# Raw w1 blocks of the first pair loaded into free x buffers, two units ahead and in program order

## The chip, the cores and the metric

The kernel runs on one core of a Trainium2 chip. A core has four engines that compute, each with a queue of its own that it works through in order: TensorE (PE, the matrix products; PEld is its weight load), VectorE (DVE), ScalarE (ACT) and GpSimd (POOL). A fifth, SyncE (SP), issues the transfers between HBM and the on-chip memory here. An engine waits at an instruction until what it reads is there and what it writes to is free, and everything behind that instruction waits with it. The metric is the device time of one execution in microseconds.

## The reference

Attention over 4 batches, 8 heads, 768 positions of 64: each query sees keys within 16 positions and 24 block summaries. Its output is laid out as 3072 tokens of 512, and goes through a mixture of four experts:

```python
p = domain_probs / (domain_probs.sum(-1, keepdims=True) + 1e-09)
for e in range(E):
    h = np.maximum(x @ w1[e], 0.0)
    out += p[:, e:e + 1] * (h @ w2[e])
```

w1 is 4 x 512 x 1024, w2 is 4 x 1024 x 512, all float32. The change concerns the loading of w1 alone.

## The kernel before

Tokens are worked in eight blocks of 384. Attention for a later block is interleaved with the experts of an earlier one. Blocks 0 and 1 go through the experts in plain products; blocks 2 to 7 go in three pairs (`PAIRS`, L926), each through all four experts, the first pair in the order 3, 2, 1, 0. In a pair the first layer of an expert (`first`, L1177) runs in four units i = 0 to 3, each with two raw blocks of w1 of 128 x 512 float32. A unit is a scheme of seven groups of six products (`SEVEN`, L1037) that write four banks of PSUM: a, d, b, a, b, c, b. Between the groups ACT copies bank a into bank b (`phb<-pha`, L1215), ACT copies d to a helper p5 (L1218), and DVE makes c (`phc`, L1220) and adds p5 to d. The second layer (`po`) of the expert ahead is interleaved with the first layer of the next; the first expert of the pair has none behind it, only attention.

The weights of a unit are made ready by `w1_operands` (L817). In the first pair it loads the two raw blocks (`wr1<e>_<block>`, by `load_weights`, L740), scales both on ACT (the page shows `one`), makes seven operands from them, each with a high part (a cast to half precision on ACT) and a low part (a subtraction on POOL or DVE), with sums between them on POOL, into two groups w1g0 and w1g1, and puts stores of both groups to HBM on a list that is issued eight units later. In the second and third pair these stored operands are loaded instead, and no raw block is touched. `fetch` (L941) walks a list of all units of all pairs and calls `w1_operands`; `first` calls it for its own unit and for the one after. `w2_scaled` (L777) does the like for w2, also with two raw blocks at a time (`wr2<e>_<block>`).

The raw blocks of w1 and of w2 share four buffers (tag `wr`). The tag `x` has 14 buffers (`NX`) of the same size. While blocks 0 and 1 run, they hold the inputs of the plain products and pieces of attention; a pair's seven operands of x take seven of them.

A scheduler sets the order of the instructions on each engine from a simulated timeline; PSUM evictions in `first` have a raised priority (`RUSH`). Loads on SP float in this order too, but for those of attention's summaries, which are pinned to the order of the program (`load_chunk`, L201, with `tc.keep_in_program_order`). In names of the profile numbers are left out: `wr` is a raw block of either layer, and its DMA names its source, `in_w1L` or `in_w2L`.

Of the kernel before, what the change touches and what calls it, by code (L numbers as in the profile page):

```python
# [8 lines left out]
F32 = mybir.dt.float32  # L9
# [7 lines left out]
P = 128  # L17
# [26 lines left out]
NX = 14  # L44
# [18 lines left out]
def attn_moe(ctx: ExitStack, tc: tile.TileContext, qvL, qv0, v0L, kD, kT, vT, w1L, w2L, dpL, cst, out):  # L63
    nc = tc.nc
# [20 lines left out]
    def pool(name, bufs=1, **kw):  # L85
        return ctx.enter_context(tc.tile_pool(name=name, bufs=bufs, **kw))
# [7 lines left out]
    sb = pool("sb")  # L94
# [645 lines left out]
    def load_weights(src, e, fc, which):  # L740
        raw = sb.tile([P, 512], F32, name=f"wr{which}{e}_{fc}", tag="wr", bufs=4)
        SP.dma_start(raw, src[e, fc])
        return raw

    def w1_parts(name, n, dtype=F32R):
        return sb.tile([P, n, 512], dtype, name=name, tag="w1", bufs=NW1)
# [5 lines left out]
    stored = {}  # L752
# [4 lines left out]
    def later(units, issue, *a):  # L757
        deferred.append([units, issue, a])
# [54 lines left out]


    WS = ("11", "s1", "s2", "12"), ("s3", "s4", "22")

    def w1_operands(e, pr):  # L817
        groups = [w1_parts(f"w1g{j}{e}_{pr}", len(names), F16) for j, names in enumerate(WS)]
        ws = {w: groups[j][:, n, :] for j, names in enumerate(WS) for n, w in enumerate(names)}
        if (e, pr, "1") in stored:  # L820
            for to, kept_in in zip(groups, stored[e, pr, "1"]):
                SP.dma_start(to, kept_in)
            return ws
        r1, r2 = (load_weights(w1L, e, 2 * pr + j, "1") for j in range(2))
        for raw in (r1, r2):
            A.mul(raw, raw, scale_w[e][0])
        a11, a12 = r1[:, 0:256], r1[:, 256:512]
        a21, a22 = r2[:, 0:256], r2[:, 256:512]
        def parts(w, raw, lo):
            hi, low = ws[w][:, 0:256], ws[w][:, 256:512]  # L830
            A.copy(hi, raw)
            lo.tensor_tensor(low, raw, hi, op=ALU.subtract)

        parts("11", a11, PL)
        parts("22", a22, V)
        PL.tensor_tensor(a22, a21, a22, op=ALU.add)
        PL.tensor_tensor(a21, a11, a21, op=ALU.subtract)
        PL.tensor_tensor(a11, a22, a11, op=ALU.subtract)
        parts("s2", a11, V)
        parts("s1", a22, PL)  # L840
        parts("s3", a21, V)
        parts("12", a12, PL)
        PL.tensor_tensor(a12, a12, a11, op=ALU.subtract)
        parts("s4", a12, V)
        stored[e, pr, "1"] = []
        for j, (names, group) in enumerate(zip(WS, groups)):
            stored[e, pr, "1"].append(dram.tile([P, len(names), 512], F16, name=f"wdg{j}{e}_{pr}"))
            later(8, SP.dma_start, stored[e, pr, "1"][j], group)
        return ws
# [82 lines left out]
    orders, todo, ready = {}, [], {}  # L932
# [8 lines left out]
    def fetch(until=None):  # L941

        while todo and until not in ready:
            *key, same = todo.pop(0)
            ready[tuple(key)] = ready[same] if same else w1_operands(*key[1:])
            if until is None and not same:
                return

# [34 lines left out]
    def with_fetch(units, places=(), early7=()):  # L983
        for n, us in enumerate(units):
            if n in (1, 8):
                fetch()
            if n in places:
                fetch2()
            if n in early7:
                fetch7()  # L990
            yield us
# [185 lines left out]
    def first(pr, tbs, e, hT, w2, room):  # L1177
# [8 lines left out]
        order = orders[pr, e]  # L1186
        for n, i in enumerate(order):
            fetch((pr, e, i))
            if n < len(order) - 1:
                fetch((pr, e, order[n + 1]))  # L1190
            elif e != es_of[pr][-1]:
                fetch()
# [179 lines left out]
```

## Time and profile before

| | |
|---|---|
| time, median of 3 runs | 1167.91 us (1165.97 to 1171.35) |
| the profiled execution | 1167.77 us, span 1166.0 us |
| mean granted clock of TensorE | 0.975 |
| transfers | 184.11 MB, mean 158 GB/s |
| raw blocks of w1 loaded | 76, 256 KB each |
| raw blocks of w2 loaded | 104, 256 KB each |

A page of the profile gives each engine's busy time and share of the span; views of the trace give the same for a stretch, the waits of an engine with what ended them, and a timeline of its instructions. A row of the timeline is start, duration, engine, operation, what it writes and reads, its shape, and in brackets the idle time just ahead and what ended it. Times are microseconds from the start of the span. The last plain first-layer product ends at about 349, the first pair's first layer begins at 390.70, and its last raw block is loaded at 590.2.

### The profile page before, as it was taken

The numbers are of one execution on the slowest core, as the hardware profiler recorded it, in microseconds if no ns is written. First come the engines' busy times: TensorE is split into PE (matmuls) and PEld (weight loads), VectorE is DVE, ScalarE is ACT, GpSimd is POOL, SyncE is SP. The second block draws the span as 40 slices with busy tenths as digits, with TensorE's granted clock in tenths as the row PEclk, the third lists the DMA queues.
The fourth block names the chain that finished last, engine by engine and source line by source line (L and its number), as shares of the span: only waits on it lengthen the run. The fifth ranks groups of instructions, "written<-read, shape, count | busy, mean of one in ns | idle before, by whom it ended". The sixth has DMA issues, their size and how long they took to land. (4 is left out here: it accounts for less than half of the span.)

```text
span 1166.0 us, 20542 instructions
## 1 busy us (share of the span) xinstructions
PE 1103.9 (95%) x6994; PEld 759.3 (65%) x6994; DVE 812.5 (70%) x1959; ACT 695.1 (60%) x1882; POOL 547.3 (47%) x650
## 2 busy tenths in 40 slices
PE   8999788999999879889979999999999999999998
PEld 6878677898897545445545555555555458686867
DVE  5888878875798666757787635556643568787783
ACT  4767476764556778787675445555532356666661
POOL 1588565773735667776663321223300134344340
PEclk9999888999999899999999999999999999999999
DMA  6477656663746667868695436465451242334201
GB/s 240 127 203 196 185 140 194 162 184 89 222 133 153 192 231 232 275 216 269 180 332 159 157 102 189 124 189 154 117 163 45 64 134 82 125 93 125 68 15 55
DMA packets 169306, 184.11 MB, mean 158 GB/s; under 512 B 79344, under 2 KB 115184, under 8 KB 169200
## 3 DMA queue, kind: packets, MB, share of 16 engines
q1 hardware_dynamic: 169200, 182.79, 51.8%
q8 instruction: 55, 0.90, 0.3%
q14 instruction: 51, 0.42, 0.1%
HBM read 131.76 MB, written 34.08 MB: 142 GB/s over the span
## 5 line engine op out<-in xcount | busy, mean ns | idle before, releaser
L75 PEld LDWEIGHTS <-w1g 128*128 128x128 f16 x2016 | 196.2, 99 | 164.7 <-issue 28.7
L75 PE MATMUL po<-w2s,h 128*128 128x512 f16 x1152 | 273.2, 381 | 1.4 <-DVE h L75 1.4
L75 PEld LDWEIGHTS <-h 128*128 128x128 f16 x1584 | 152.9, 98 | 128.0 <-issue 4.7
L75 PE MATMUL phb<-x_t,w1g 128*128 128x384 f16 x864 | 166.0, 329 | 14.5 <-DVE phc L75 7.2
L75 PE MATMUL ph<-xh,w 128*128 128x384 f32 x512 | 144.0, 352 | 10.0 <-ACT xh L75 3.8
L75 POOL TENSOR_TENSOR ks<-kr,ks 128x304 fp32r<-128x304 f32 x112 | 99.7, 895 | 101.2 <-ACT ks L75 100.3
L75 PE MATMUL pha<-x,w1g 128*128 128x384 f16 x576 | 116.0, 336 | 7.8 <-DVE nb L75 4.8
L75 PE MATMUL po<-w,hh 128*128 128x512 f32 x384 | 122.1, 397 | 0.0
L75 ACT ACTIVATE ms<-ms,nb 96x152 f32<-96x152 f32 x256 | 104.3, 415 | 25.1 <-DVE nb L75 24.2
L75 POOL TENSOR_TENSOR w<-wr,w 128x512 fp32r<-128x512 f32 x60 | 82.4, 1382 | 53.2 <-ACT w L75 47.9
L75 PEld LDWEIGHTS ph<-xh,w 128*128 128x128 f32 x512 | 97.8, 197 | 12.3 <-ACT xh L75 4.2
L75 DVE CUSTOM_DVE_ANT_0 ms<-psc,c_sb 96x152 f32<-96x152 f32 x256 | 69.3, 305 | 37.6 <-PE psc L75 33.3
L75 POOL TENSOR_TENSOR v<-qv,v 128x256 f16<-128x256 f32 (+1 forms) x56 | 42.4, 759 | 103.7 <-ACT v L75 91.3
L75 PE MATMUL ph<-xl,w 128*128 128x384 f32 x256 | 89.0, 348 | 0.0
L75 PEld LDWEIGHTS po<-w,hh 128*128 128x128 f32 x384 | 70.8, 189 | 14.5
L75 PE MATMUL po<-w,hl 128*128 128x512 f32 x192 | 76.4, 399 | 0.0
L75 POOL TENSOR_TENSOR w2g<-wr,w2g 128x256 f16<-128x256 f32 (+1 forms) x32 | 29.5, 938 | 99.6 <-ACT w2g L75 99.4
L75 DVE TENSOR_TENSOR aw<-ms,aw 96x512 f16<-96x512 f32 x112 | 68.2, 642 | 8.7 <-ACT aw L75 8.6
L75 ACT CAST aw<-ms 96x512 f16<-96x512 f32 x112 | 49.5, 488 | 41.2 <-issue 20.1
L75 ACT CAST w<-wr 128x512 fp32r<-128x512 f32 x84 | 51.0, 616 | 30.5 <-DMA wr<-in_w1L 18.5
L75 PE MATMUL psc<-ks,qs 128*96 128x152 f32 x448 | 64.2, 268 | 5.0 <-POOL qs L75 4.6
L75 ACT CAST ks<-kr 128x304 fp32r<-128x304 f32 x112 | 48.2, 442 | 31.7 <-PE psc L75 31.0
(184 smaller groups left out, 2241.6 us busy)
## 6 DMA issues: line engine op xcount, KB each, us to landing
wr<-in_w2L SPq DMA_DIRECT2D x104, 256.0 KB, 3.2
wr<-in_w1L SPq DMA_DIRECT2D x76, 256.0 KB, 3.2
qv<-in_qvL SPq DMA_DIRECT2D x56, 320.0 KB, 3.6
kr<-in_kD SPq DMA_DIRECT2D x56, 256.0 KB, 3.2
w1g<-wdg SPq DMA_DIRECT2D x28, 512.0 KB, 3.6
w1g<-wdg SPq DMA_DIRECT2D x28, 384.0 KB, 3.6
wdg<-w1g SPq DMA_DIRECT2D x16, 512.0 KB, 3.9
wd<-w2s SPq DMA_DIRECT2D x16, 512.0 KB, 4.6
```

The costliest lines, as they stand in the source:

```text
L75: ins = getattr(self.engine, name)(*a, **kw)
```

## The change

A dictionary `raw_w1` and a function `load_raw` are added. `load_raw` takes two tiles `wx<e>_<block>` from the tag `x` and loads the two raw blocks of a unit into them, pinned to the order of the program on SP. `w1_operands` takes these in place of tiles of `wr`. `fetch`, after each unit that it makes ready, calls `load_raw` for the next two entries of its list, as long as the entry that it made ready belongs to the first pair; entries whose operands are stored already, or that use those of an earlier unit again, are passed over. The raw blocks of w2 keep the four `wr` buffers for themselves.

```diff
@@ -813,6 +813,16 @@
 
 
     WS = ("11", "s1", "s2", "12"), ("s3", "s4", "22")
+    raw_w1 = {}
+
+    def load_raw(e, pr):
+        if (e, pr) in raw_w1 or (e, pr, "1") in stored:
+            return
+        raw_w1[e, pr] = []
+        for j in range(2):
+            raw = sb.tile([P, 512], F32, name=f"wx{e}_{2 * pr + j}", tag="x", bufs=NX)
+            tc.keep_in_program_order(nc.sync.dma_start(raw, w1L[e, 2 * pr + j]))
+            raw_w1[e, pr].append(raw)
 
     def w1_operands(e, pr):
         groups = [w1_parts(f"w1g{j}{e}_{pr}", len(names), F16) for j, names in enumerate(WS)]
@@ -821,7 +831,8 @@
             for to, kept_in in zip(groups, stored[e, pr, "1"]):
                 SP.dma_start(to, kept_in)
             return ws
-        r1, r2 = (load_weights(w1L, e, 2 * pr + j, "1") for j in range(2))
+        load_raw(e, pr)
+        r1, r2 = raw_w1.pop((e, pr))
         for raw in (r1, r2):
             A.mul(raw, raw, scale_w[e][0])
         a11, a12 = r1[:, 0:256], r1[:, 256:512]
@@ -943,6 +954,9 @@
         while todo and until not in ready:
             *key, same = todo.pop(0)
             ready[tuple(key)] = ready[same] if same else w1_operands(*key[1:])
+            for _, e, i, again in todo[:2]:
+                if key[0] == 1 and not again:
+                    load_raw(e, i)
             if until is None and not same:
                 return
```

The order on the engines moves from the end of the plain experts to the start of the second pair; elsewhere it stays. First SP, where the raw blocks of the first units stand (`wr13_0` and `wx3_0` are block 0 of expert 3; `vch`, `kr`, `qv` and `awT` belong to attention, `xd` takes a piece of its output to HBM). Before:

```order
L203 DMA vch2_1_3996<-in_vT 128x768
L75 DMA wr13_0_4659<-in_w1L 128x512
L75 DMA wr13_1_4661<-in_w1L 128x512
L203 DMA vch2_2_4000<-in_vT 128x768
L75 DMA wr13_2_4904<-in_w1L 128x512
L75 DMA wr13_3_4906<-in_w1L 128x512
L75 DMA kr34_4262<-in_kD 128x4x128
L203 DMA vch2_3_4004<-in_vT 128x768
```

After, 16 rows further down, while `wr23` blocks (w2 of expert 3) stand in the old places:

```order
L75 DMA xd1_3_2981<-xs30_4334 128x192
L824 DMA wx3_0_4659<-in_w1L 128x512
L75 DMA_TRANSPOSE awT32_4422<-aw0_732 128x12x96
L824 DMA wx3_1_4661<-in_w1L 128x512
L75 DMA xd1_3_2981<-xs31_4499 128x192
L824 DMA wx3_2_4685<-in_w1L 128x512
L824 DMA wx3_3_4687<-in_w1L 128x512
L824 DMA wx3_4_4689<-in_w1L 128x512
L824 DMA wx3_5_4691<-in_w1L 128x512
L75 DMA_TRANSPOSE awT33_4619<-aw0_732 128x12x96
```

The four blocks of the first two units have moved behind two transposes of attention's probabilities, and the third unit's two (`wx3_4`, `wx3_5`) follow at once. The next piece is SP again, at the start of the pair. Before:

```order
L75 DMA qv38_5033<-in_qvL 128x640
L75 DMA_TRANSPOSE awT35_4996<-aw0_732 128x12x96
L75 DMA xd2_1_5057<-xs34_5054 128x192
L75 DMA wr23_0_5155<-in_w2L 128x512
L75 DMA wdg03_0_4683<-w1g03_0_4657 128x2048
L75 DMA wr23_1_5160<-in_w2L 128x512
L75 DMA kr39_5190<-in_kD 128x4x128
L75 DMA qv39_5191<-in_qvL 128x640
L75 DMA out_dram<-acc3_2377 128x512
L75 DMA wdg03_1_4928<-w1g03_1_4902 128x2048
L75 DMA wdg13_0_4684<-w1g13_0_4658 128x1536
```

After:

```order
L75 DMA wr23_5_5439<-in_w2L 128x512
L75 DMA wd23_0_5172<-w2s3_0_5162 128x2048
L75 DMA out_dram<-acc3_2377 128x512
L75 DMA out_dram<-acc4_2379 128x512
L75 DMA wr23_6_5541<-in_w2L 128x512
L75 DMA_TRANSPOSE awT35_5004<-aw0_732 128x12x96
L824 DMA wx3_7_4936<-in_w1L 128x512
L75 DMA out_dram<-acc5_2381 128x512
L75 DMA wd23_1_5304<-w2s3_1_5294 128x2048
L75 DMA wdg03_0_4683<-w1g03_0_4657 128x2048
L75 DMA wr23_7_5546<-in_w2L 128x512
```

The eighth raw block, `wx3_7`, is pinned with three stores and a w2 load close behind it, and the transpose awT35 stands behind more w2 loads and two stores of finished tokens (`out_dram`) that were behind it before. Now ACT, from the copy of the first unit of the pair, `phb1_3_0`. Before, the second unit's copy is eight rows down:

```order
L75 COPY phb1_3_0_5126<-pha1_3_0_5119 128x384
L75 ACTIVATE qv39_5191<-qv39_5191,vscale2_4028 128x256
L75 COPY p51_3_0_5135<-phd1_3_0_5128 128x384
L75 CAST v12_38_5355<-qv38_5033 128x4x64
L75 ACTIVATE xs35_5297<-px35_5165 128x192
L75 CAST ks38_0_5346<-kr38_5032 128x2x152
L75 ACTIVATE ms37_5178,rs37_5180<-ms37_5178,nb37_5179 96x152 x2
L75 ACTIVATE h2_3_0_5151<-pha1_3_0_5119 128x384
L75 COPY phb1_3_1_5257<-pha1_3_1_5250 128x384
```

After, it is 27 rows down, and these are the first twelve:

```order
L75 COPY phb1_3_0_5134<-pha1_3_0_5127 128x384
L75 ACTIVATE wr23_6_5541<-wr23_6_5541,scalew3_4599 128x512
L75 CAST w1g03_1_4910<-wx3_2_4685 128x256
L75 COPY p51_3_0_5143<-phd1_3_0_5136 128x384
L75 CAST v12_38_5363<-qv38_5041 128x4x64
L75 ACTIVATE xs35_5305<-px35_5173 128x192
L75 ACTIVATE wx3_7_4936<-wx3_7_4936,one3_4606 128x512
L75 CAST w1g13_0_4658<-wx3_0_4659 128x256
L75 CAST w2s3_3_5540<-wr23_6_5541 128x512
L75 CAST aw0_732<-ms36_5028 96x512
L75 CAST aw0_732<-ms36_5028 96x4x2x24
L75 CAST w1g13_2_5231<-wx3_5_4691 128x256
```

In between stand scaling and casts of w1 and w2 blocks of later units (`wx3_7`, `w1g03_1`, `w2s3_3`) that came later before. Last PE, at the start of the pair's first layer. Before, the scores of attention's step 36 (`psc36`) stand inside the second layer (`po1_3`) of the last plain expert:

```order
L75 MATMUL po1_3_2_4947<-w23_5_4426,hh1_3_5_4418 128x512 x2
L75 MATMUL po1_3_2_4947<-w23_5_4426,hl1_3_5_4419 128x512
L75 MATMUL psc36_1_5059<-ks36_1_4968,qs36_4971 96x152 x4
L75 MATMUL po1_3_0_4945<-w23_6_4514,hh1_3_6_4495 128x512 x2
L75 MATMUL po1_3_0_4945<-w23_6_4514,hl1_3_6_4496 128x512
```

After, they stand behind it:

```order
L75 MATMUL po1_3_2_4955<-w23_7_4581,hh1_3_7_4575 128x512 x2
L75 MATMUL po1_3_2_4955<-w23_7_4581,hl1_3_7_4576 128x512
L75 MATMUL psc36_0_5031<-ks36_0_4973,qs36_4979 96x152 x4
L75 MATMUL psc36_1_5067<-ks36_1_4976,qs36_4979 96x152 x4
L75 LDWEIGHTS w1g03_0_4657
L75 MATMUL phd1_3_0_5136<-x1_t1_4624,w1g03_0_4657 128x384
```

The two products of scores have moved from within the second layer to right ahead of the first unit's first products, which now begin with bank d (`phd1_3_0`) and not with bank a.

## The prediction

> **What bounds the kernel now.** I read the whole-program rows first, then three stretches around the start of the first pair of blocks, then TensorE's own gaps there, and last what ACT stood waiting for.
>
> ```profile
> span 1166.0 us, 20542 instructions
> PE 1103.9 (95%) x6994; PEld 759.3 (65%) x6994; DVE 812.5 (70%) x1959; ACT 695.1 (60%) x1882; POOL 547.3 (47%) x650
> ```
>
> TensorE is busy for 1103.9 of 1166.0 us. The change takes away none of its products, so it can only win idle time of TensorE, 62 us over the whole program, and time at a low clock. The profiled execution took 1167.77 us, 1.8 above its span and 0.14 below the median of the three runs, 1167.91; the sum below starts from 1167.77.
>
> ```profile
> 375.00:440.00 65.00, 52.89 (x307) 32.96 (x306) 44.81 (x111) 48.42 (x133) 42.31 (x54) 0.92 0.65 206
> 440.00:606.00 166.00, 152.91 (x885) 81.98 (x886) 118.60 (x264) 127.60 (x342) 116.21 (x138) 0.98 0.76 246
> 606.00:700.00 94.00, 92.31 (x531) 49.27 (x531) 57.22 (x161) 44.88 (x142) 31.27 (x44) 0.95 0.49 155
> ```
>
> Columns: the stretch, its length, busy us of PE, weight loads, DVE, ACT and POOL, the granted clock, the DMA share, GB/s. The raw blocks of w1 are needed between 375 and 606, while the first pair runs. TensorE is idle there for 12.1 + 13.1 = 25.2 us, and that is all the change can reach directly. In the first stretch ACT is busy 48.42 of 65 us and in the second 127.60 of 166, about 75%: it isn't idle enough to be ignored.
>
> TensorE's gaps in the first expert of the pair:
>
> ```profile
> 397.91 0.57 PE L75 MATMUL psc<-ks,qs 128*96 128x152 f32 x4 [4.63 <-POOL qs L75]
> 399.60 2.08 PE L75 MATMUL phb<-x_t,w1g 128*128 128x384 f16 x6 [1.11 <-ACT phb L75]
> 425.52 2.21 PE L75 MATMUL pha<-x,w1g 128*128 128x384 f16 x6 [2.07 <-ACT w1g L75]
> ```
>
> The number in brackets is the wait ahead of the row and what ended it. The largest, 4.63, ends on attention work on POOL (qs), not on a weight; the third ends on a w1 operand cast by ACT. Its cause is one row back on ACT:
>
> ```profile
> 424.45 0.72 ACT L75 ACTIVATE wr<-wr,one 128x512 f32<-128x512 f32 x1 [3.76 <-DMA wr<-in_w1L]
> ```
>
> ACT, in order, stood 3.76 us at a raw block that had not landed. This is the wait that an earlier load takes away.
>
> **The change, part by part.** *Loads.* The count is the same: each raw block is still 256 KB and read once. What moves is the place in SP's queue and the buffer. The first four w1 blocks don't come earlier: their rows move behind two attention transposes, because the x buffers come free only after the last plain product. That costs nothing as long as `one`, the scale, is what ACT waits for, and in before it was: ACT scaled those four in one run with no wait in brackets:
>
> ```profile
> 379.79 2.56 ACT L75 ACTIVATE wr<-wr,one 128x512 f32<-128x512 f32 x4
> ```
>
> From the third unit on, w1 blocks stand in the queue two units ahead, and the w2 blocks have the four wr buffers to themselves.
>
> *First expert (units phb1_3_0 to phb1_2_1).* ACT issues one copy, phb<-pha, per unit. Between the first unit's copy and that of the fifth unit after it before has 91 rows in its order, after 113.
>
> ```profile
> 399.07:452.83 53.76, 40.85 (x107) 0.91 0.77 252
> ACT wr L75 <- DMA wr<-in_w1L: 6.4, 3, 3.8
> ACT qv L75 <- DMA qv<-in_qvL: 2.4, 1, 2.4
> ACT h L75 <- DVE phd L75: 1.9, 2, 1.0
> ACT w2s L75 <- DMA wr<-in_w2L: 0.7, 1, 0.7
> ```
>
> The stretch between the two copies took 53.76 us, of which ACT worked 40.85 and waited 12.9. 6.4 + 0.7 = 7.1 of that is weight loads; 5.8 is other things (2.4 for a qv load, 1.9 for DVE, 1.5 in small pieces). The 22 rows that ACT does in addition, because work of later units can now be done sooner:
>
> ```profile
> L75 ACT CAST w1g<-wr 128x256 f16<-128x256 f32 x33 | 12.2, 399 | 2.8 <-POOL wr L75 2.8
> L75 ACT ACTIVATE wr<-wr,scalew 128x512 f32<-128x512 f32 x3 | 2.2, 726 | 0.7 <-DMA wr<-in_w2L 0.7
> ```
>
> Twelve casts of w1g at 0.40, one scaling of a w1 block, three of w2 blocks and two products of like size at about 0.7, and four smaller ones at 0.4 to 0.5: 4.8 + 4.2 + 1.9 = 10.9. Rows that follow each other on ACT overlap by some 0.1 us (before's stretch has a cast of 0.40 starting at 451.90 and the next row at 452.21), so 8.9 of time.
>
> ```profile
> 451.90 0.40 ACT L75 CAST w1g<-wr 128x256 f16<-128x256 f32 x1
> 452.21 0.72 ACT L75 ACTIVATE w2s<-wr,scalew 128x512 f16<-128x512 f32 x1
> ```
>
> ACT then needs 40.85 + 8.9 = 49.75 us where it had 53.76. I take the first copy 0.4 later than before: in after the scores of step 36 go ahead of the first product and hold its bank, which gives TensorE three new waits of about 3.1, 2.7 and 0.4 us, 6.2 where there were 4.63 + 1.11 = 5.74. (These are my estimates, from walking the new order with the old durations.) So the fifth copy comes at best 53.76 - 49.75 - 0.4 = **3.6 us earlier**. If ACT keeps all 5.8 us of its other waits, it comes 2.2 **later**. The waits for DVE and PE (about 3) fall away when ACT is the late one; the qv load was issued late behind weight loads and now stands ahead of them. I take 1.1 of the 5.8 and so **-2.5 us**; bounds -3.6 and +2.2. What is late next is ACT itself: it has almost no slack left in this stretch.
>
> *The other three experts of the pair.* TensorE's gaps there, and ACT's waits just ahead of them:
>
> ```profile
> 473.77 3.18 PE L75 MATMUL po<-w2s,h 128*128 128x512 f16 x14 [1.36 <-DVE h L75]
> 489.73 1.29 PE L75 MATMUL phb<-x_t,w1g 128*128 128x384 f16 x6 [2.46 <-DVE phd L75]
> 523.58 1.14 PE L75 MATMUL phb<-x_t,w1g 128*128 128x384 f16 x6 [3.46 <-DVE phc L75]
> 553.56 1.14 PE L75 MATMUL phb<-x_t,w1g 128*128 128x384 f16 x6 [0.74 <-ACT phb L75]
> 600.41 1.14 PE L75 MATMUL phb<-x_t,w1g 128*128 128x384 f16 x6 [1.34 <-ACT phb L75]
> 607.62 2.08 PE L75 MATMUL pha<-x,w1g 128*128 128x384 f16 x6 [4.78 <-DVE nb L75]
> ```
>
> ```profile
> 467.90 0.72 ACT L75 ACTIVATE wr<-wr,one 128x512 f32<-128x512 f32 x1 [1.65 <-DMA wr<-in_w1L]
> 520.25 0.72 ACT L75 ACTIVATE w2s<-wr,scalew 128x512 f16<-128x512 f32 x1 [1.31 <-DMA wr<-in_w2L]
> 551.44 0.72 ACT L75 ACTIVATE wr<-wr,scalew 128x512 f32<-128x512 f32 x1 [1.38 <-DMA wr<-in_w2L]
> 599.26 0.72 ACT L75 ACTIVATE w2s<-wr,scalew 128x512 f16<-128x512 f32 x1 [1.21 <-DMA wr<-in_w2L]
> ```
>
> Each of four gaps (1.36, 3.46, 0.74, 1.34: 6.9 us) stands a few us behind an ACT wait for a raw block; the second goes by way of DVE, whose w2s subtraction waits for that ACT row. The gaps of 2.46 and 4.78 are attention's reductions and maxima on DVE, and no load stands behind them; I leave them in. The 22 ACT rows that went into the first expert are missing here, so ACT gets 8.9 us easier, and the loads are up to two units ahead. I take two thirds of 6.9: **-4.6 us**; bounds 0 (the loads stay late, or POOL, which makes the w1 sums, becomes the wait) and -6.9.
>
> *The clock.*
>
> ```profile
> 427.00:429.00 2.00, 2.00 (x8) 0.50 0.05 20
> 491.00:493.00 2.00, 2.00 (x15) 0.50 0.67 147
> 525.00:527.00 2.00, 2.00 (x7) 0.50 0.97 296
> ```
>
> The granted clock (third from last) is 0.50 after the gaps of 2.07, 2.46 and 3.46 us: even a gap of 2 us near other small ones is followed by some 3 to 4 us at half speed, about 1.7 us lost each time. Two of the three (2.07 and 3.46) are load waits. Half of these 3.4 goes, **-1.7**; bounds 0 and -3.4. The 4.63 at the start is split into 3.1 and 2.7, which by the 2.46 row is no protection, so I count nothing for it.
>
> The Trainium skill, "TensorE: Matmul & The Clock Gate", Part 1, has the clock halve only after an idle window of about 3.4 us. By that rule the split at the start would leave the clock at full speed and some 2.6 us more would be won (an estimate from that page, 1158.9). This case's trace disagrees: 2.46 us were enough for 0.50.
>
> *New waits.* wx3_7 is the fifteenth tile in fourteen buffers: it can only be issued when the first unit's raw block has been read for the last time, and its program order is fixed, so it stands in SP's queue with the out stores, w2 loads and the next transpose behind it. In the walk it is issued at about 398 and needed at about 402, so with a landing of 3.2 us it is just in time. Each later unit has the same shape. No row of before shows this wait. From below it is nothing; from above it is 28.0 us in 14 waits, what SP waits for DVE's aw in this region, which is hidden there for the most part. I take **+2.0**, one wait of that size on the path; bounds 0 and +4.
>
> ```profile
> SPq L75 <- DVE aw L75: 28.0, 14, 6.9
> wr<-in_w1L SPq DMA_DIRECT2D x76, 256.0 KB, 3.2
> ```
>
> DVE's two rows fewer and ACT's two more move nothing.
>
> *Sum:* -2.5 - 4.6 - 1.7 + 2.0 = -6.8, so 1167.77 - 6.8 = **1161.0 us**.
>
> **Rivals.**
>
> *More is won.* All terms at their good ends: -3.6 - 6.9 - 3.4 + 0 = -13.9, 1153.9 us. For it speaks that loads end most of ACT's idle time in 375 to 606; against it that ACT has under 4 us of slack left and that a new order of the engines always brings some waits of its own.
>
> *The wait only changes its name.* ACT stays the bound in the first expert with its other waits kept in part (term 0 instead of -2.5), and in the later experts only the two gaps that end directly on ACT's copy go (0.74 + 1.34 = 2.1), no clock, new waits +2: 1167.8 - 2.1 + 2.0 = 1167.7. For it: the largest gaps (4.63, 4.78) are not load waits, POOL and DVE are behind ACT in a chain, and 25.2 us of idle time have many owners.
>
> *Slower: ACT's early weight work goes ahead of the copies that TensorE waits for.* Place: between phb1_3_0 and phb1_3_1 there were 7 other rows on ACT and are now 26. Those rows take some 11 us back to back, where before the two copies were 6.4 apart (399.07, the start of the window above, and the row below); six of them are casts of w1 parts, five of which read a sum made by POOL. Price: ACT keeps its 5.8 us of waits (+2.2 at the fifth copy), the extra casts wait like those of this region, 10.5 us in 14 waits or 0.75 each, five times (+3.8), and SP's fixed order costs its upper +4; nothing is won later but 4.6. That is 1167.8 + 2.2 + 3.8 + 4.0 - 4.6 = 1173.2. It decides from the point where ACT waits over 3.6 us in the stretch; it is slower in total when that passes 3.6 + 4.6.
>
> ```profile
> 405.48 0.46 ACT L75 COPY phb<-pha 128x384 f32<-128x384 f32 x1 [0.62 <-PE pha L75]
> ACT w1g L75 <- POOL wr L75: 10.5, 14, 2.3
> ```
>
> The Trainium skill, "DMA: Bandwidth & Descriptors", Anatomy of one DMA, has any semaphore wait happen on the issuing sequencer before dispatch; by that a pinned load whose buffer is busy stops everything behind it on SP, which is this rival's last term. The trace agrees: SP's queue shows the waits quoted above.
>
> *The change doesn't do what it says.* For the first unit this is so already: its loads stand later in the queue than before. If the x buffers came free late for all units, w1 blocks would land as late as now; the time would be before's, 1167 to 1169. The pair keeps 7 of the 14 buffers for its own operands, so six raw blocks fit: little speaks for it.
>
> **How the numbers follow.** Forecast (1157 to 1164) 0.40; more is won (below 1157) 0.15; the wait changes its name, or the loads don't come earlier (1164 to 1171) 0.25; slower (above 1171) 0.20. The range takes in the forecast, most of the first rival and about half of the last: 1152 to 1174.5, which leaves out about 0.06 below and 0.11 above. Half a per cent, 5.8 us, is about what a measurement of this kernel can tell from no change: below 1162.0 lie all of the first rival and about three quarters of the forecast, 0.15 + 0.30 = 0.45; above 1173.6 lies some two thirds of the slow case, 0.14; 0.41 is between.
>
> **What would show it.**
>
> ```profile
> ACT wr L75 <- DMA wr<-in_w1L: 18.3, 13, 3.8
> ```
>
> This row of ACT's waits between 380 and 610 falls to under 5; if it doesn't, the loads aren't early. TensorE's gap before the fourth unit (2.07, ended by w1g) is gone; the gaps at 523 and 600 are gone or under 1 us. The copy phb of the second expert's second unit comes at about 450 instead of 452.83; if it comes after 453, ACT was the bound. SP's row of waits for x buffers (ended by DVE or POOL's last read of wx) stays under 2 us each. After 620 both traces run alike, shifted by the gain. Wrong would be: TensorE's idle time between 375 and 606 at 25 us or more, with ACT phb or POOL w1 sums as the releaser.

## The result, and the profile after

| | before | changed |
|---|---|---|
| median | 1170.65 us (15 runs, 1165.97 to 1174.85) | 1163.23 us (15 runs, 1160.62 to 1168.51) |
| ratio, 95% interval | | 0.9948 [0.9931, 0.9964] |
| profiled execution | 1167.77 us, span 1166.0 | 1163.23 us, span 1161.5 |

The changed kernel is faster by 0.52%, or 6.1 us of 1170.65 by the ratio; 1161.0 was forecast from 1167.77, 6.8 us. The medians lie 7.4 us apart and the two profiled executions 4.5, because the profiled execution of before was 2.9 faster than the median of its 15 runs. The page of the changed kernel begins:

```profile
span 1161.5 us, 20511 instructions
PE 1102.4 (95%) x6994; PEld 758.6 (65%) x6994; DVE 818.6 (70%) x1959; ACT 692.7 (60%) x1882; POOL 550.8 (47%) x650
```

TensorE's work is the same to 1.5 us; the span loses 4.5 us, most of it idle time. The three stretches of the prediction, with the same columns, in the changed kernel:

```profile
375.00:440.00 65.00, 54.14 (x295) 33.67 (x294) 55.02 (x107) 57.63 (x156) 60.17 (x71) 0.87 0.84 262
440.00:606.00 166.00, 156.27 (x917) 85.02 (x914) 122.09 (x285) 121.27 (x337) 109.83 (x132) 0.96 0.71 234
606.00:700.00 94.00, 90.72 (x537) 48.16 (x537) 54.82 (x146) 42.89 (x131) 27.19 (x39) 0.99 0.47 138
```

Between 375 and 606 TensorE is idle for 10.9 + 9.7 = 20.6 us instead of 25.2; after 606 it is idle for 3.3 instead of 1.7. In the first stretch POOL works 60.17 of 65 us where it worked 42.31, ACT 57.63 for 48.42, DVE 55.02 for 44.81: weight work has moved forward into the first expert, and POOL is nearly full there. TensorE's larger gaps in the first expert of the changed kernel:

```profile
393.60 1.56 PE L75 MATMUL psc<-ks,qs 128*96 128x152 f32 x8 [3.64 <-POOL qs L75]
397.21 2.08 PE L75 MATMUL pha<-x,w1g 128*128 128x384 f16 x6 [1.38 <-DVE nb L75]
400.71 1.46 PE L75 MATMUL phd<-x_t,w1g 128*128 128x384 f16 x4 [1.43 <-POOL w1g L75]
403.36 0.45 PE L75 MATMUL px<-awT,v 128*64 128x192 f16 x4 [1.19 <-DMA awT<-aw]
417.10 2.08 PE L75 MATMUL phb<-x_t,w1g 128*128 128x384 f16 x6 [1.41 <-ACT phb L75]
```

The gap of 2.07 that ended on a w1 operand is gone; the start of the pair is worse (3.64 + 1.38 + 1.43 + 1.19 = 7.64 us where there were 4.63 + 1.11). The larger gaps from the second expert to the end of the stretch:

```profile
522.27 2.02 PE L75 MATMUL phb<-x_t,w1g 128*128 128x384 f16 x6 [2.75 <-DVE phd L75]
595.75 0.56 PE L75 MATMUL psc<-ks,qs 128*96 128x152 f32 x4 [2.20 <-DVE nb L75]
599.06 2.08 PE L75 MATMUL pha<-x,w1g 128*128 128x384 f16 x6 [2.75 <-DVE nb L75]
```

All four gaps of before that the prediction put down to a load are gone, and so is the 2.46 at 489.73 that it put down to attention. The 2.75 at 522.27 is new. It stands in the same unit as the 3.46 of before, and no load is behind it: DVE, which had no wait just there, made attention's `aw` ahead of `phd`. The gaps at the end wait for DVE's maxima of attention's scores (`nb`), as the 4.78 at 607.62 of before did; with two more of 0.65 they come to 6.25.

The second layer goes tile by tile in the same order in both kernels, so DVE's accumulations of it are milestones. From DVE's timeline, four of before and then the same four of the changed kernel:

```profile
473.64 0.73 DVE L75 TENSOR_SCALAR acc<-po,pw 128x512 f32<-128x512 f32 x1
549.52 0.74 DVE L75 SCALAR_TENSOR_TENSOR acc<-po,pw,acc 128x512 f32<-128x512 f32 x1
606.03 0.73 DVE L75 SCALAR_TENSOR_TENSOR acc<-po,pw,acc 128x512 f32<-128x512 f32 x1
655.12 0.73 DVE L75 SCALAR_TENSOR_TENSOR acc<-po,pw,acc 128x512 f32<-128x512 f32 x1
```

```profile
470.19 0.74 DVE L75 TENSOR_SCALAR acc<-po,pw 128x512 f32<-128x512 f32 x1
539.74 0.74 DVE L75 SCALAR_TENSOR_TENSOR acc<-po,pw,acc 128x512 f32<-128x512 f32 x1
596.09 0.73 DVE L75 SCALAR_TENSOR_TENSOR acc<-po,pw,acc 128x512 f32<-128x512 f32 x1
651.11 0.74 DVE L75 SCALAR_TENSOR_TENSOR acc<-po,pw,acc 128x512 f32<-128x512 f32 x1
```

The changed kernel is ahead by 3.5, 9.8, 9.9 and 4.0 us. So some 6 us are won between the first row and the second, and some 6 given back by the fourth. After that both traces run alike. What TensorE did from the second row to the fourth, in before and in the changed kernel (the columns are the stretch, its length, busy us of PE, the granted clock, the DMA share and GB/s):

```profile
549.52:655.12 105.60, 98.67 (x575) 0.95 0.69 220
539.74:651.11 111.37, 101.85 (x596) 0.95 0.64 204
```

The changed kernel takes 5.8 us longer there. 2.6 of that is idle time of TensorE (9.5 us against 6.9) and 3.2 is work: some 20 products more, which before had done ahead of its second row. Part of the lead at that row was work put off.

One profile cannot carry a difference of 3 us here. TensorE's order is the same in all kernels of this study up to the last plain first-layer product, and the last matmul of that product with xh begins at 348.74 in before and at 347.56 in the changed kernel; in the profiles of the experiments it is between 346.16 (e6) and 353.67 (e12). The times of the experiments are therefore ratios over several executions, and a lead in a profile is better counted from this one, the common product: the changed kernel's is then 2.3, 8.6, 8.7 and 2.8 us at the four rows, and 3.3 at the end.

### The profile page after: what moved, and what is told of

It reads as the page before. It is cut to its first block, busy times and chain, and to the rows that moved or that the text cites. A ratio compares the mean times of both kernels' runs of the same rounds, so it can differ in the third digit from the quotient of the medians.

```text
span 1161.5 us, 20511 instructions
## 1 busy us (share of the span) xinstructions
PE 1102.4 (95%) x6994; PEld 758.6 (65%) x6994; DVE 818.6 (70%) x1959; ACT 692.7 (60%) x1882; POOL 550.8 (47%) x650
## 4 chain that ended last, share of the span: by engine, by line
PE 37%; DVE 6%; DMA 4%; ACT 2%; issue 2%; POOL 1%; SPq 0%; POOLq 0%; ACTq 0%; DVEq 0%
PE po L75 14%; PE phb L75 8%; PE pha L75 5%; PE phc L75 3%; PE phd L75 3%; DVE wr L75 2%; PE poa L75 1%; PE pob L75 1%; PE psc L75 1%; DMA wr<-in_w2L 1%; DVE acc L75 1%; DMA kch<-in_kT 1%; PE pod L75 1%; PE px L75 1%; DMA vch<-in_vT 1%
## 5 line engine op out<-in xcount | busy, mean ns | idle before, releaser
L75 PEld LDWEIGHTS ph<-xh,w 128*128 128x128 f32 x512 | 97.9, 197 | 13.4 <-ACT xh L75 4.2
```

What stands on the lines that cost most here:

```text
L75: ins = getattr(self.engine, name)(*a, **kw)
```

## The experiments

Twelve kernels, each run several times beside the kernel before on the same chip.

| | w1 buffers | look-ahead | pinned | ratio | 95% interval | ACT's waits for raw w1, us |
|---|---|---|---|---|---|---|
| the change | x | 2 | yes | 0.9948 | 0.9931 to 0.9964 | 12.4 |
| e1 | x for experts 2, 1, 0 | 2 | yes | 1.0026 | 1.0004 to 1.0048 | 14.0 |
| e2 | x for expert 3 | 2 | yes | 1.0037 | 1.0014 to 1.0061 | 15.4 |
| e3 | x | 0 | yes | 1.0071 | 1.0040 to 1.0102 | 15.9 |
| e4 | x | 2 | no | 0.9932 | 0.9906 to 0.9959 | 6.0 |
| e5 | x for experts 3, 2, 1 | 2 | yes | 0.9904 | 0.9880 to 0.9928 | 9.8 |
| e6 | x | 1 | yes | 1.0027 | 1.0002 to 1.0052 | 16.2 |
| e7 | x | 3 | yes | 0.9929 | 0.9903 to 0.9954 | 8.7 |
| e8 | shared tag; w2 takes x | none | no | 0.9978 | 0.9963 to 0.9994 | 12.3 |
| e9 | x | 0 | no | 0.9908 | 0.9873 to 0.9944 | 7.5 |
| e10 | x | 1 | no | 0.9902 | 0.9870 to 0.9933 | 6.8 |
| e11 | x for experts 3, 2, 1 | 2 | no | 0.9924 | 0.9896 to 0.9953 | 4.4 |
| e12 | x | 0 | not expert 0 | 1.0007 | 0.9990 to 1.0023 | 13.4 |

The last column is what ACT waited for raw blocks of w1 between 380 and 610 in the profile (the rows of `wr` and `wx` together; before has 18.3). The six kernels at 0.9932 and below waited 4.4 to 9.8 us, the other seven 12.3 to 16.2. Within each group the order of the waits is not that of the times, so the wait goes with the gain and does not measure it.

**Which experts.** e1 and e2 each keep one half of the change.

```diff
# e1, in w1_operands and fetch
+        if e == es_of[1][0]:
+            raw_w1[e, pr] = [load_weights(w1L, e, 2 * pr + j, "1") for j in range(2)]
         load_raw(e, pr)
...
-                if key[0] == 1 and not again:
+                if key[0] == 1 and not again and e != es_of[1][0]:
# e2: the same two conditions the other way round
```

> The first expert of the pair (expert 3) loads its raw w1 blocks as before, from the four shared buffers; only experts 2, 1 and 0 of the pair have x buffers and two units of look-ahead. Theory A (the gain is made in experts 2 and 1, where ACT's waits for raw blocks held TensorE up; the first expert only loses time because ACT and POOL are full there): faster than before by 0.5% or more, ratio 0.990 to 0.995, with TensorE's start of the first expert as before (first copy phb at about 399, second at about 405). Rival B (the look-ahead in the first expert builds the stock of ready weights that the later experts live on): most of the gain is gone, ratio 0.997 to 1.000.

> The opposite half: only expert 3 has x buffers and look-ahead, experts 2, 1 and 0 load from the shared four as before. Theory A: no gain, ratio 0.998 to 1.004, and ACT's waits for in_w1L come back after 440 (over 8 us). Rival B: most of the gain is kept, ratio 0.994 to 0.997.

Measured: 1.0026 and 1.0037. Both halves alone are slower than before, and both theories fall: the gain is neither in the later experts alone nor in a stock that the first one builds (1.0037 lies in the range that theory A gave e2, but e1 contradicts that theory). Both kernels still have the pin, which the next runs show to be a cost. Counted from the common product, e1's profile is still 0.8 us ahead of before at the third milestone (606.52) and 5.5 behind at the fourth (661.97): it loses in expert 0, which it handles as the change does. e2 is 3.2 behind at the first milestone already and 6.2 at the third. Why was not tried further and stays open.

**Look-ahead and pin.** e3 takes the look-ahead away, e4 the pin.

```diff
# e3
-            for _, e, i, again in todo[:2]:
+            for _, e, i, again in todo[:0]:
# e4
-            tc.keep_in_program_order(nc.sync.dma_start(raw, w1L[e, 2 * pr + j]))
+            SP.dma_start(raw, w1L[e, 2 * pr + j])
```

> The x buffers and the pin stay, but no block is loaded ahead of the call that needs it (which is one unit ahead of the products anyway). Theory A with look-ahead as the cause: ACT waits for in_w1L again (over 10 us between 380 and 610), ratio 0.998 to 1.002. Rival C (what counts is that w1 and w2 no longer share four buffers): the gain stays, ratio 0.993 to 0.996, and the look-ahead is worth nothing.

> As the change, with the loads of w1 left to the scheduler instead of pinned to program order. If the pin costs time because blocked loads stop SP's queue: faster than the change by 2 to 4 us, ratio to before 0.990 to 0.993. If the pin is without effect, the same as the change, 0.994 to 0.996. If the pin is what brings the loads early: slower than the change, 0.997 or above.

Measured: 1.0071 and 0.9932. Without look-ahead the pinned kernel is 8 us slower than before, so the pin alone does not bring the loads early. e4 is not clear of the change (the intervals overlap), so the pin beside two units of look-ahead costs little or nothing that can be measured.

**Expert 0, the distance, and the other weights.**

```diff
# e5
+        if e == es_of[1][-1]:
+            raw_w1[e, pr] = [load_weights(w1L, e, 2 * pr + j, "1") for j in range(2)]
         load_raw(e, pr)
...
-                if key[0] == 1 and not again:
+                if key[0] == 1 and not again and e != es_of[1][-1]:
# e6 and e7: todo[:1] and todo[:3] for todo[:2]
# e8, in w2_scaled of the kernel before
-                raw = load_weights(w2L, e, 2 * j + n, "2")
+                raw = sb.tile([P, 512], F32, name=f"wr2{e}_{2 * j + n}", tag="x", bufs=NX)
+                SP.dma_start(raw, w2L[e, 2 * j + n])
```

> As the change for experts 3, 2 and 1 of the pair; the last one, expert 0, loads its raw w1 blocks from the shared four without look-ahead, as before. In the changed kernel the gain stands at some 10 us at the end of expert 1 and falls to 4 in expert 0. Theory D (the give-back belongs to the weight work of expert 0 that comes earlier and pushes attention's last scores together): faster than the change, ratio to before 0.988 to 0.992. Rival E (the give-back is only attention catching up: whatever was won ahead of it is lost where TensorE waits for DVE): the same as the change, 0.993 to 0.997. If expert 0 needs its loads early as the others do: slower than the change, 0.998 or more.

> The change with one unit of look-ahead instead of two. No look-ahead measured 1.007, two units 0.995. If the look-ahead works by its distance (blocks land before ACT comes to them): between, 0.998 to 1.003. If one unit is enough to cover a landing of some 3 us: 0.993 to 0.997.

> The change with three units of look-ahead: eight raw blocks for seven free buffers, so the last blocks of the look-ahead have to wait for a buffer, pinned in SP's queue with everything behind them. If distance is what counts: 0.990 to 0.994. If a pinned load that waits for a buffer costs time: 0.997 to 1.005. If two units hide all there is to hide: as the change, 0.993 to 0.997.

> The kernel before with one edit: the raw w2 blocks of the pair take x buffers, w1 keeps the four shared ones for itself; no look-ahead, no pin. Rival C (w1 and w2 sharing four buffers is the cost, however it is ended): 0.993 to 0.997. If look-ahead of w1 is the cause: no gain, 0.998 to 1.008, and ACT still waits over 10 us for in_w1L between 380 and 610.

Measured: 0.9904, 1.0027, 0.9929, 0.9978. With the pin, no, one, two and three units of look-ahead give 1.0071, 1.0027, 0.9948 and 0.9929: the distance counts. Two units are clear of one and of none; none and one, and two and three, have intervals that overlap. e5 is faster than the change, with intervals that only just don't meet (0.9928 and 0.9931). Its third milestone, and TensorE's largest gap there:

```profile
600.47 0.73 DVE L75 SCALAR_TENSOR_TENSOR acc<-po,pw,acc 128x512 f32<-128x512 f32 x1
602.74 1.12 PE L75 MATMUL pha<-x,w1g 128*128 128x384 f16 x3 [5.97 <-DVE nb L75]
541.07:650.32 109.25, 98.87 (x590) 0.97 0.69 214
```

The first row of e5 answers to 606.03 of before and 596.09 of the change. e5 had reached the common product 3.1 us later than before (351.83), the change 1.2 earlier. Counted from there e5 is 8.7 us ahead at this row and 7.9 at the fourth (650.32), the change 8.7 and 2.8. So e5 gives back next to nothing between these two rows. It doesn't do so by removing the wait for `nb`: its gap is 5.97 us, and its idle time from the second milestone to the fourth (the third row above) is 10.4 us, no less than the change's 9.5. Of the 5.1 us by which e5 leads the change at the fourth row, 3.0 stand at the second already, where the change has the gap at 522.27 and its half clock and e5 has neither. The times show, if by little, that the way the change loads expert 0 costs something; by which wait stays open. One trace of it: the profile's chain of work that ended last runs in the change, while expert 0 is worked, through two transposes of attention's probabilities, and in e4 and e5 through none. Start, duration and what:

```profile
611.20 4.18 DMA awT<-aw
616.94 3.02 DMA awT<-aw
```

e8 shows that four buffers for w1 alone, with w2 in the x buffers, give 0.2%, with ACT's wait for in_w1L at 12.3 us.

What the pin does without look-ahead can be seen in SP's queue of e3. These rows are from its timeline, the last v chunk of attention and the last raw blocks of expert 0, and TensorE's largest gap there:

```profile
603.60 0.33 SPq L203 DMA_DIRECT2D vch<-in_vT  x1
617.72 1.56 SPq L824 DMA_DIRECT2D wx<-in_w1L  x2
624.11 1.05 SPq L824 DMA_DIRECT2D wx<-in_w1L  x2
```

```profile
610.98 0.37 PE L75 MATMUL pmx<-c_sb,vm 128*1 128x128 f32 x1 [5.97 <-DVE vm L75]
```

Attention's chunks are pinned too (L203), so the pin puts both kinds of load in one order: e3's last four blocks are issued behind the four v chunks. In before the last raw block went out at 590.23, in the changed kernel at 573.35. The gap of 5.97 doesn't wait for those blocks (after 610 ACT waits 0.3 us for w1 in e3). It waits for DVE's `vm`, made from the v chunks. That TensorE stands there with nothing else to do because the products of expert 0 have no weights yet is argued, not shown.

**Without the pin.** e9 and e10 take the pin away from e3 and e6, e11 from e5.

```diff
# e9: e3 with the line of e4; e10: todo[:1] with it; e11: e5 with it
-            tc.keep_in_program_order(nc.sync.dma_start(raw, w1L[e, 2 * pr + j]))
+            SP.dma_start(raw, w1L[e, 2 * pr + j])
```

> x buffers for the raw w1 blocks, no look-ahead, no pin: the least that can be left of the change. In e3 and e6 the pin put the last four or two raw blocks of expert 0 behind the four pinned v chunks of attention, and they were loaded at 617 to 624 instead of 590; without the pin the order has them ahead again. Theory F (look-ahead counts only because the pin ties w1's loads to attention's; the seven free buffers are the gain): as the kernel with look-ahead and no pin, 0.991 to 0.996, a gain over e3 of 11 us or more. Rival: look-ahead counts by itself, the loads come too late without it: 1.000 to 1.008 as in e3.

> One unit of look-ahead, no pin. Theory F: 0.991 to 0.996, the same as with none and with two. Rival (distance counts): halfway between e3 and e4, 0.997 to 1.003.

> The two edits that measured best, together: no pin, and expert 0 loading as before. If their gains add up (0.0016 for the pin, 0.0044 for expert 0, against the change at 0.9948): 0.987 to 0.991. If both remove the same loss in expert 0: as e5, 0.989 to 0.993.

Measured: 0.9908, 0.9902, 0.9924. e9 differs from e3 by the pin alone, and is 1.6% faster, 19 us. Without the pin no, one and two units give 0.9908, 0.9902 and 0.9932: no distance can be told any more. e11, at 0.9924, does not add the gains of e4 and e5. That fits one loss that both take away, but e4's gain over the change is not clear of noise to begin with. SP's row of the last raw block in e9:

```profile
541.09 0.33 SPq L75 DMA_DIRECT2D wx<-in_w1L  x1
```

That is 49 us ahead of before and 32 ahead of the change. In e10 and e4 it is at 541.83 and 543.11. Left alone, the scheduler puts this load in the same place whether it is asked to look ahead or not.

**Where the pin costs.** e12 pins all but expert 0.

```diff
# e12, beside e3
-            tc.keep_in_program_order(nc.sync.dma_start(raw, w1L[e, 2 * pr + j]))
+            load = nc.sync.dma_start(raw, w1L[e, 2 * pr + j])
+            if e != es_of[1][-1]:
+                tc.keep_in_program_order(load)
```

> As e3 (x buffers, no look-ahead, pinned), but for expert 0 of the pair, whose raw blocks float. Theory F with its place (the pin costs where expert 0's blocks stand behind attention's pinned v chunks): as e9, 0.988 to 0.996. If the pin costs in every expert: 1.000 to 1.008, as e3. In the trace the last raw blocks of expert 0 are issued before 590 and not at 617 to 624.

Measured: 1.0007, at the low end of the second range, but not as e3. The last raw blocks go out at 572.35, ahead of the v chunks, as expected. Against e3 (1.0071, intervals apart) the pin in expert 0 costs 0.6%, about 7 us; against e9 (0.9908, apart too) the pin in the other three costs another 1.0%, about 12 us. In the profiles 7.3 us of the latter stand between the second and the third milestone (548.27 to 609.64 in e12, 542.42 to 596.55 in e9). The place named is one part of the cost, not the whole.

## Why the prediction was right, and where its reasons were not

*The sum.* -6.8 us forecast, -6.1 measured. By the milestones, counted from the common product, 2.3 us are won up to the first (the first expert's term: 2.5) and 6.3 up to the second (the later experts and the clock: 4.6 + 1.7); then 5.8 are given back, where 2.0 were put for new waits. In these two profiles the whole is -3.3. That the ratio comes so near the forecast is luck in part: the give-back was undersized, and before's profiled execution, from which the sum starts, was a fast one.

*First expert, -2.5 (bounds -3.6 and +2.2).* The term failed at its own mark, the fifth copy: it comes at 457.30, 4.5 later than the 452.83 of before. The prediction's window, from the first copy to that one, in the changed kernel, and ACT's waits in it:

```profile
403.48:457.30 53.82, 48.66 (x131) 0.94 0.97 326
ACT w1g L75 <- POOL wx L75: 3.6, 5, 1.2
ACT aw L75 <- DVE ms L75: 1.6, 1, 1.6
```

ACT's work was sized well (49.75 forecast, 48.66 measured) and its waits for loads are gone from the window, as said. But 5.2 us of waits stay, most of them for POOL's w1 sums, where 1.1 had been taken; POOL is busy for 52.09 us of this window. And the first copy comes 4.4 later, not 0.4. ACT's timeline around it, and the second copy:

```profile
398.60 0.51 ACT L75 ACTIVATE qv<-qv,vscale 128x256 f32<-128x256 f32 x1 [2.24 <-DMA qv<-in_qvL]
403.48 0.47 ACT L75 COPY phb<-pha 128x384 f32<-128x384 f32 x1
416.58 0.47 ACT L75 COPY phb<-pha 128x384 f32<-128x384 f32 x1
```

The products that the first copy reads end at 399.3. ACT stood 2.24 us for attention's qv load and then worked without a gap up to the copy. The forecast counted TensorE's waits and had this load come in time; its wait has only moved out of the window. At the first milestone the kernel is none the worse for it, 2.3 us ahead, with some 25 products fewer done by then (620 since the common product, 645 in before).

*The other three experts, -4.6.* Right in kind: the gaps that it named are gone. That loads had caused them was argued from nearness in time, and the 6.3 us won from the first to the second milestone were not all won there. The 2.46 that the prediction left in went too, and 2.75 came in at 522.27.

*The clock, -1.7.* About right in size, but not in its places. These are the stretches at half clock (third from last) from 375 to 655, five of before and four of the changed kernel:

```profile
398.42:405.24 6.82, 5.71 (x19) 0.50 0.99 331
425.72:429.14 3.42, 3.33 (x12) 0.50 0.32 119
490.58:493.99 3.41, 3.41 (x19) 0.50 0.84 240
524.71:528.12 3.41, 3.41 (x12) 0.50 1.00 339
606.63:616.87 10.24, 9.18 (x35) 0.50 0.79 280
```

```profile
392.66:406.31 13.65, 8.72 (x39) 0.50 0.98 292
416.56:419.97 3.41, 2.87 (x10) 0.50 1.05 409
522.37:525.78 3.41, 3.41 (x18) 0.50 0.92 227
597.46:607.70 10.24, 7.24 (x27) 0.50 0.59 213
```

TensorE works 25.0 us at half clock in before and 22.2 in the changed kernel; half of the difference, 1.4 us, is an estimate of what the clock gives. The stretch behind the 2.07 is gone, as forecast, but 416.56 is new in the same expert, and the one behind the 3.46 has a successor. The one that went besides stood behind the 2.46, which was to stay. The one at the start, for which nothing was counted, is twice as long: the first wait was not split into 3.1 and 2.7 but is 3.64 in one piece, with three smaller ones behind it. (The other time that the prediction gives for the split, 1158.9, should read 1158.4, 1161.0 less 2.6.)

*New waits, +2.0.* Mis-sized and misplaced. They were put on SP, behind wx3_7. That block was issued at 400.68 (398 forecast), and its scaling on ACT at 405.70 did not wait. The give-back is 5.8 us from the second milestone to the fourth, 2.6 of it in waits and 3.2 in work put off, and most of it falls where attention's last scores meet expert 0. e5 shows that it is smaller when expert 0 loads as before, though the wait for DVE's `nb` stays.

*What was to be seen.* ACT's wait for in_w1L was to fall from 18.3 to under 5. In the changed kernel:

```profile
ACT wx L75 <- DMA wx<-in_w1L: 12.4, 7, 3.1
ACT w1g L75 <- POOL wx L75: 13.6, 20, 2.6
SPq L824 <- POOL w1g L75: 3.6, 2, 2.9
```

It is 12.4, and all of it falls in the later experts. SP's waits for an x buffer, which were to stay under 2 us each, reach 2.9 (third row). Of the other signs, the gaps before the fourth unit and at 600 are gone, and the one at 523 has its successor of 2.75; the fifth copy is late; TensorE's idle time fell below 25 us; both traces run alike from 655 on. The largest wait of the first row, from ACT's timeline, with the load's row from SP's:

```profile
542.29 0.72 ACT L75 ACTIVATE wx<-wx,one 128x512 f32<-128x512 f32 x1 [3.11 <-DMA wx<-in_w1L]
539.22 1.05 SPq L824 DMA_DIRECT2D wx<-in_w1L  x2
```

The pinned pair is issued 3.1 us ahead of ACT's scaling, so ACT does wait, but no gap of TensorE over 1 us stands there: ACT's wait isn't lost time in this place. In the kernels that load without the pin the row falls to 4.4 to 7.5 us.

*The cause.* The prediction put the gain on the loads being two units ahead in program order. The runs show the other half of the edit at work: seven buffers for w1 alone where it shared four, unpinned and without look-ahead (e9), give 0.9908. The pin takes from that (e3, 1.0071), and the look-ahead gives most of it back (0.9948). Separation by itself gives little (e8). More buffers in the shared tag were not tried.

*The rivals.* The slower one named ACT's crowded first expert and SP's fixed order. Both exist. The first two copies are 13.1 us apart (403.48 and 416.58), where some 11 were feared and before has 6.4; but TensorE's order has other products between them, and the gap that ends on the second copy is 1.41 (417.10). The fixed order makes the kernel slower than before with less look-ahead (e3, e6). With two units it is mostly covered.

*A version that beats both:* e10 (0.9902), e9 (0.9908) and e5 (0.9904) are the fastest measured, and not told apart by these runs; e5 and the change have intervals that don't meet, e9's and e10's touch the change's.

## What to carry to other kernels

Where a scheduler places loads by itself, give it free buffers first and measure that alone; a pin or a look-ahead by hand is a second edit with a cost of its own, and two groups of loads that are pinned on one queue are pinned to each other. A gain won in one stage is worth what the next stage can take: follow milestones that are in the same order in both traces through to the end, and look where the lead shrinks. Before explaining 3 us between two profiles, see how far apart they are where their instructions are still the same.

## What the runs showed of the hardware

With the same order of TensorE's instructions up to there, the same matmul is reached up to 7.5 us apart in different executions (346.16 to 353.67, in these two rows of the timelines of e6 and e12). The two ran on different chips; e5, on the chip of e6, is at 351.83. On SP both have the order of before up to a v chunk that is issued at 315.02 in e6 and at 322.62 in e12, and on the other engines for longer, so the spread is there before the orders part:

```profile
346.16 0.33 PE L75 MATMUL ph<-xh,w 128*128 128x384 f32 x1
353.67 0.33 PE L75 MATMUL ph<-xh,w 128*128 128x384 f32 x1
```

And the granted clock (third from last) was again halved after a gap of under 3 us, here the 2.75 us ahead of 522.27 in the changed kernel. The nine stretches at half clock that are listed above last 3.41, 6.82, 10.24 or 13.65 us, one to four times 3.41:

```profile
523.00:525.00 2.00, 2.00 (x14) 0.50 0.95 186
```
